# An S4 layer with a gated feed-forward net, forward and backward: powers only at the positions that bf16 leaves distinct, four channels per product, crossbar transposes, stored pre-activations

## The chip, the cores and the metric

The kernel runs on one core of one Trainium2 chip. The metric is the device time of one execution in microseconds (us). The engines are PE (matrix multiply, with its weight loads counted apart as PEld), DVE (vector engine), ACT (scalar engine), POOL, and SP, which here only issues DMAs. "Granted clock" is the share of full speed that PE was allowed; with a low one matmuls take longer.

## The reference

The forward function and the gradients of all its inputs are to be computed, for L = 2048 positions, D = 512 channels, N = 128 states and F = 1792 hidden units. Cut to what matters:

```python
def ssm(u, A, B, C, log_dt, Dskip):
    dt = exp(log_dt)[:, None]
    l  = arange(L).astype(bfloat16)                  # the argument turns on this line
    P  = exp((dt * A)[:, :, None] * l)               # complex powers, D x N x L
    K  = einsum("dn,dnl,dn->dl", C, P, dt * B).real  # convolution kernel, D x L
    y  = irfft(rfft(pad(u)) * rfft(pad(K)))[:L]      # causal convolution, padded to 4096
    return y + u * Dskip
xn  = layernorm(x)
out = x + ssm(xn, ...) * silu(silu(xn @ w1) @ w2)
# outputs: out, and the gradients of x, A, B, C, log_dt, Dskip, w1, w2
```

The positions are rounded to bf16, so not all 2048 are distinct: 0 to 256 are exact, then come steps of 2, 4 and 8, with 128 values each. 257 + 3 x 128 = 641 are left.

## The kernel before

It never stores the powers of all positions. It writes each power as a product of a table X (a coarse step) and a table Y (a fine step), and K is then a matmul over the states. Two channels share one 128-column product. The same tables are needed transposed for the backward pass, so PE transposes them, ACT and DVE evacuate the results, and they go through DRAM (XTD, YTD). Per group of eight channel pairs, 32 groups in all:

```python
    X = ck.tile([P, 4, QCH, 64, 2], BF16, name="Xc")
    outer_pform(nc, X, H["XH"], H["XL"], H["XLn"], c0, QCH)       # 4 DVE products
    for qb in range(0, QCH, 2):                                   # transposes of X, on PE
        pf = psum.tile([P, 2, 2, P], F32, name="pf_t")
        ...  nc.tensor.matmul(out=pf[:, qi, c, :], lhsT=X[:, 2 * c, qb + qi]..., rhs=k.ident[:], ...)
        nc.scalar.copy(out=XT[:, qb:qb + 2], in_=pf[:])           # XTf, on ACT
    nc.sync.dma_start(k.XTD[:, q0:q0 + QCH], XT[:])
    YY = ...; outer_cplx(nc, ck, YY[:, 0]..., ...)                # 6 DVE products
    ...  # transposes of YY (pt_t), evacuated by DVE (YTf), stored to YTD
    for qi in range(8):
        for m in range(4):
            nc.tensor.matmul(out=ps[:, qi]..., lhsT=X[:, m, q]..., rhs=YY[:, m // 2, q, 32:64, :]...)   # ps_k
    nc.scalar.activation(out=tmpP[:, 1, :, qa:qa + 8].rearrange("p j q -> p q j"), in_=ps[:, :, :, 1], ...)  # kf_tmpP
    nc.scalar.activation(out=tmpP[:, 0, :, qa:qa + 8].rearrange("p j q -> p q j"), in_=ps[:, :, :, 0], ...)
```

The convolution is a discrete Fourier transform (DFT) in two matmul steps with a transpose between them. In this kernel PE does that transpose:

```python
    ...                                         # first step: PSUM -> A (tile dftA)
    for c in range(2):
        for g0 in range(0, G, 8):
            pt = psumT.tile([P, 8, 128], BF16, name="pt_b")
            for gi in range(8):
                nc.tensor.transpose(out=pt[:, gi, :], in_=A[:, c, g0 + gi, :, :]..., identity=ident[:])
            EV(nc, B[:, c, g0:g0 + 8, :], pt[:])
    ...                                         # second step: B -> X
```

The backward pass of the feed-forward net computes the first product again and takes silu and tanh of it:

```python
    for dk in range(DK):
        nc.tensor.matmul(out=ps_h[:], lhsT=XNT[:, dk, t, :], rhs=W1[:, dk, fs], ...)     # ps_hb, 256 matmuls
    for dk in range(DK):
        nc.tensor.matmul(out=ps_da[:], lhsT=DOT_s[:, dk, :], rhs=W2T[:, dk, fs], ...)
    nc.scalar.activation(out=a_s[:, fs], in_=ps_h[:], func=ACT.Silu)
    nc.scalar.activation(out=th[:], in_=ps_h[:], func=ACT.Tanh, scale=0.5)
```

## Time and profile before

| | before |
|---|---|
| time, median of 2 | 1344.2 us (1342.22 to 1346.17) |
| profiled span | 1348.3 us |
| PE / DVE / ACT busy | 893 / 894 / 744 us |
| DMA packets, of which under 512 B | 333,686, 287,890 |

The page of the kernel before, parts 1 and 2. Part 1 gives busy time, share of the span and instructions of each engine. In part 2 each digit is the busy share, in tenths, of one of 40 equal slices of the span (33.7 us here); PEclk is the granted clock in tenths.

```profile
PE 893.1 (66%) x8258; PEld 580.6 (43%) x8314; DVE 894.4 (66%) x1490; ACT 744.2 (55%) x1217; POOL 9.4 (1%) x50
## 2 busy tenths in 40 slices
PE   1486850376767674666676666288788888646997
...
DVE  7177877597989894494756748187777777857100
ACT  5779887285646455547475565255555555541111
```

No engine is full on average. The limit changes with the stage, which the view by stretches shows. Its columns are the window and its length in us, then the busy us and the instructions of PE, PEld, DVE, ACT and POOL, the granted clock, the DMA share and GB/s.

```profile
0.00:255.00 255.00, 119.07 (x557) 55.34 (x568) 159.13 (x249) 192.15 (x279) 9.35 (x50) 0.85 0.28 102
255.00:520.00 265.00, 189.77 (x2700) 160.82 (x2701) 239.22 (x388) 157.84 (x216) 0.00 (x0) 0.85 0.50 154
520.00:849.00 329.00, 212.45 (x1940) 135.88 (x1959) 203.80 (x221) 189.46 (x304) 0.00 (x0) 0.87 0.26 59
849.00:1348.00 499.00, 371.81 (x3061) 228.51 (x3086) 292.28 (x633) 204.79 (x420) 0.00 (x0) 0.84 0.75 171
```

The first row is setup, the exponent tables and the feed-forward net. The second holds the tables: DVE is busy 239 of 265 us. The third holds the convolutions, where no engine passes 65%: a chain of steps that wait for each other. The fourth is the backward pass of the feed-forward net and of the state space model (SSM).

The groups view of the kernel before, for what the change removes. Columns: source line, engine, operation, output<-inputs, shapes, count | busy us, mean ns of one | idle us of the engine just before them, and what ended that idle time.

```profile
L620 PE MATMUL pf_t<-ident_bfloat_87,Xc 128*128 128x128 bf16 x512 | 84.4, 247 | 96.1 <-DVE Xc L344 72.9
L622 ACT CAST XTf<-pf_t 128x512 bf16<-128x512 f32 x128 | 74.0, 658 | 26.1 <-PE pf_t L621 12.5
L645 ACT ACTIVATE kf_tmpP<-ps_k,odd 128x256 bf16<-128x256 f32 x32 | 45.4, 1420 | 78.0 <-PE ps_k L642 76.5
L896 PE MATMUL ps_hb<-W_291,XNT 128*128 128x448 bf16 x256 | 60.7, 355 | 3.1 <-ACT Vb L779 1.9
```

The third line writes only 256 elements per partition and takes 1420 ns, while XTf writes 512 in 658 ns. kf_tmpP writes each element alone, far from the last one.

### The profile page before, as it was taken

Reading aid. Unit: us, or ns where it says so; the run is one execution under the profiler, and the core shown is the slowest. Engines: PE = TensorE matmul, PEld = TensorE weight load, DVE = VectorE, ACT = ScalarE, POOL = GpSimd, SP = SyncE. Lnnn points to the kernel's source line nnn. Section 1 sums busy time; section 2 is a strip of 40 time slices with the busy share of each in tenths; the row PEclk is TensorE's granted clock in tenths of the full one; section 3 lists DMA queues with packets and bytes.
Section 4 is the critical chain, followed back from the end, with each engine's and each line's share of the span. In section 5 each row is a group of like instructions: output and inputs, shape, how many; then the busy total and the mean of one; then the engine's idle time right before and its main releaser. Section 6 shows DMA issues by size and latency. Waiting matters only on the chain. (4 is left out here: it accounts for less than half of the span.)

```text
span 1348.3 us, 20797 instructions
## 1 busy us (share of the span) xinstructions
PE 893.1 (66%) x8258; PEld 580.6 (43%) x8314; DVE 894.4 (66%) x1490; ACT 744.2 (55%) x1217; POOL 9.4 (1%) x50
## 2 busy tenths in 40 slices
PE   1486850376767674666676666288788888646997
PEld 0232320266656563334354443144444444333487
DVE  7177877597989894494756748187777777857100
ACT  5779887285646455547475565255555555541111
POOL 0000000000000000000000000000000000000000
PEclk9999985587888887889898888598888898856999
DMA  3112312546463736442411102977686877897744
GB/s 129 59 62 86 133 67 89 206 158 210 125 195 103 204 110 146 97 94 47 94 33 32 32 1 46 221 160 184 150 185 153 178 168 180 156 171 211 176 130 117
DMA packets 333686, 171.90 MB, mean 127 GB/s; under 512 B 287890, under 2 KB 300052, under 8 KB 333076
## 3 DMA queue, kind: packets, MB, share of 16 engines
q1 hardware_dynamic: 179348, 102.65, 28.5%
q10 hardware_dynamic: 154240, 67.91, 20.3%
q8 instruction: 65, 1.06, 0.3%
q14 instruction: 33, 0.27, 0.1%
HBM read 93.19 MB, written 77.33 MB: 126 GB/s over the span
## 5 line engine op out<-in xcount | busy, mean ns | idle before, releaser
L620 PE MATMUL pf_t<-ident_bfloat_87,Xc 128*128 128x128 bf16 x512 | 84.4, 247 | 96.1 <-DVE Xc L344 72.9
L620 PEld LDWEIGHTS <-Xc 128*128 128x128 bf16 x512 | 54.3, 112 | 80.6 <-issue 69.9
L645 ACT ACTIVATE kf_tmpP<-ps_k,odd 128x256 bf16<-128x256 f32 x32 | 45.4, 1420 | 78.0 <-PE ps_k L642 76.5
L622 ACT CAST XTf<-pf_t 128x512 bf16<-128x512 f32 x128 | 74.0, 658 | 26.1 <-PE pf_t L621 12.5
L779 ACT CAST Vb<-psV 128x512 bf16<-128x512 f32 x128 | 67.1, 594 | 29.8 <-PE psV L777 23.3
L621 PE MATMUL pf_t<-ident_bfloat_87,Xc 128*128 128x128 bf16 x512 | 79.3, 245 | 4.2 <-DVE Xc L347 3.5
L922 PE MATMUL ps_dx<-W1T,dhT 128*128 128x512 bf16 x204 | 66.4, 472 | 7.0 <-ACT dhT L184 4.7
L770 DVE TENSOR_TENSOR Gbd<-Gt,MK 128x512 bf16<-128x512 bf16 x64 | 43.4, 687 | 37.5 <-PE psV L777 36.0
L621 PEld LDWEIGHTS <-Xc 128*128 128x128 bf16 x512 | 54.1, 112 | 31.9 <-issue 23.0
L524 PE MATMUL ps_h<-XNT,W_291 128*128 128x512 bf16 x217 | 55.8, 407 | 16.8 <-ACT th L538 9.5
L899 PE MATMUL ps_da<-W2T,DOT_s 128*128 128x448 bf16 x256 | 60.9, 358 | 7.8 <-ACT DOT_s L184 3.7
L633 PE MATMUL pt_t<-ident_bfloat_87,YY 128*64 128x128 bf16 x512 | 49.0, 252 | 23.5 <-DVE YY L331 14.1
L896 PE MATMUL ps_hb<-W_291,XNT 128*128 128x448 bf16 x256 | 60.7, 355 | 3.1 <-ACT Vb L779 1.9
L642 PE MATMUL ps_k<-YY,Xc 128*128 128x64 bf16 x1024 | 48.8, 207 | 15.4 <-ACT kf_tmpP L646 14.8
L646 ACT ACTIVATE kf_tmpP<-ps_k,even 128x256 bf16<-128x256 f32 x32 | 51.8, 1619 | 5.5 <-DVE YTf L634 5.5
L534 PE MATMUL ps_o<-W_440,aT 128*128 128x512 bf16 x220 | 49.8, 379 | 4.8 <-ACT aT L526 4.5
L633 PEld LDWEIGHTS <-YY 128*64 128x64 bf16 x512 | 38.3, 129 | 33.2 <-DVE YY L331 17.5
L777 PE MATMUL psV<-XT,Gbd 128*128 128x256 bf16 x256 | 48.6, 330 | 5.8 <-DVE Gbd L770 2.6
L642 PEld LDWEIGHTS <-Xc 128*128 128x128 bf16 x1024 | 42.8, 107 | 21.2 <-issue 16.9
L974 PEld LDWEIGHTS <-xn 128*128 128x128 bf16 x512 | 48.9, 98 | 4.1 <-issue 2.2
L114 PE MATMUL pt_b<-ident_bfloat_87,dftA 128*128 128x128 bf16 x384 | 31.5, 238 | 28.3 <-ACT dftA L26 14.8
L634 DVE COPY YTf<-pt_t 64x1024 bf16<-64x1024 bf16 x64 | 41.8, 680 | 11.9 <-PE pt_t L633 7.3
(2228 smaller groups left out, 2558.9 us busy)
## 6 DMA issues: line engine op xcount, KB each, us to landing
XTD<-XTf SPq DMA_DIRECT2D x32, 512.0 KB, 3.3
XT<-XTD SPq DMA_DIRECT2D x32, 512.0 KB, 4.3
YTD<-YTf ACTq DMA_DIRECT2D x32, 256.0 KB, 2.9
YT<-YTD SPq DMA_DIRECT2D x32, 256.0 KB, 4.0
YT<-YTD ACTq DMA_DIRECT2D x32, 256.0 KB, 4.8
Ad<-a_s SPq DMA_DIRECT2D x16, 448.0 KB, 3.3
DHd<-dh_s ACTq DMA_DIRECT2D x16, 448.0 KB, 4.3
A_ft<-Ad SPq DMA_DIRECT2D x7, 512.0 KB, 4.0
```

Source lines behind the costliest of these rows:

```text
L524: nc.tensor.matmul(out=ps[:], lhsT=W1[:, dk, ft * P:(ft + 1) * P], rhs=XNT[:, dk, 4 * tcn:4 * tcn + 4, :], start=(dk == 0), stop=(dk == DK ...
L534: nc.tensor.matmul(out=pso[:], lhsT=aT[:, ft, tt * P:(tt + 1) * P], rhs=W2[:, ft, :], start=(ft == 0), stop=(ft == FT - 1))
L620: nc.tensor.matmul(out=pf[:, qi, c, :], lhsT=X[:, 2 * c, qb + qi].rearrange("p a b -> p (a b)"), rhs=k.ident[:], start=True, stop=False)
L621: nc.tensor.matmul(out=pf[:, qi, c, :], lhsT=X[:, 2 * c + 1, qb + qi].rearrange("p a b -> p (a b)"), rhs=k.ident[:], start=False, stop=True)
L622: nc.scalar.copy(out=XT[:, qb:qb + 2], in_=pf[:])
L633: nc.tensor.transpose(out=pt[0:64, qi, c, :], in_=YY[:, c, qb + qi, 0:32, :].rearrange("p j e -> p (j e)"), identity=k.ident[:])
L642: nc.tensor.matmul(out=ps[:, qi].rearrange("p j e -> p (j e)"), lhsT=X[:, m, q].rearrange("p a b -> p (a b)"), rhs=YY[:, m // 2, q, 32:64, ...
L646: nc.scalar.activation(out=tmpP[:, 0, :, qa:qa + 8].rearrange("p j q -> p q j"), in_=ps[:, :, :, 0], func=ACT.Copy, scale=k.even[:, 0:1])
L779: nc.scalar.copy(out=Vb[:, qb:qb + 2], in_=psV[:])
L896: nc.tensor.matmul(out=ps_h[:], lhsT=XNT[:, dk, t, :], rhs=W1[:, dk, fs], start=(dk == 0), stop=(dk == DK - 1))
L899: nc.tensor.matmul(out=ps_da[:], lhsT=DOT_s[:, dk, :], rhs=W2T[:, dk, fs], start=(dk == 0), stop=(dk == DK - 1))
L922: nc.tensor.matmul(out=ps_dx[:], lhsT=dhT[:, ft, :], rhs=W1T[:, ft, :], start=(ft == 0), stop=(ft == FT - 1))
```

## The change

The intent is to do less of everything in the tables: powers at 641 positions only (21 coarse exponents E and 32 fine steps Y per channel), four channels in one 128-row product instead of two, no transposes on PE (the crossbar of the DMA does them, in the DFT too), no recomputed first product (pre-activations are stored and loaded), and a new form of the SSM sums. It is a rewrite; this is its core, with cuts marked:

```diff
+E_EXP = [256 * i for i in range(1, 9)] + list(range(8)) + [258, 260, 262, 516, 772]
+Y_EXP = [8 * j for j in range(1, 8)] + [64, 128, 192]
 ...  # gen_tables, per half block of 64 channels
-    outer_pform(nc, X, H["XH"], H["XL"], H["XLn"], c0, QCH)
-    ...  (pf_t, XTf, XTD; outer_cplx; pt_t, YTf, YTD)
+    V = tbl.tile([P, 2, 8, 64], I32, name="V", tag="tv")          # phase; single buffer
+    ...
+    nc.scalar.activation(out=sn[:, :, 0:n], in_=V[:, :, 0:n], func=ACT.Sin, ...)
+    TT(out=..E.., in0=qe(sn[...]), in1=qe(mag[...]), op=ALU.mult)
+    nc.sync.dma_start(k.Ed[b, h], E[:]...)
+    ...  # Y from its exponents, stored to Yd; W = E times C
+    for q in range(8):
+        for m in range(4):
+            nc.tensor.matmul(out=ps[:, q // 4, (q % 4) * 84:(q % 4) * 84 + 84],
+                             lhsT=Y[:, m // 2, q0 + q]..., rhs=W[:, m, q]..., start=(m == 0), stop=(m == 3))
+    for u in range(2):
+        k.evk(Xr[:, :, :, qq + 4 * u:qq + 4 * u + 4].rearrange("p a e q -> p q e a"),
+              ps[:, u, 0:336].rearrange("p (q e a) -> p q e a", e=NE, a=4))
 ...  # dft_fwd
-            for gi in range(8):
-                nc.tensor.transpose(out=pt[:, gi, :], in_=A[:, c, g, :, :]..., identity=ident[:])
-            EV(nc, B[:, c, g0:g0 + 8, :], pt[:])
+    nc.sync.dma_start_transpose(B[:].rearrange("p c g k -> p (c g) k"), A[:].rearrange("p c g t e -> p (c g t e)"))
 ...  # backward of the feed-forward net
-                nc.tensor.matmul(out=ps_h[:], lhsT=XNT[:, dk, t, :], rhs=W1[:, dk, fs], ...)
-            nc.scalar.activation(out=a_s[:, fs], in_=ps_h[:], func=ACT.Silu)
+                nc.sync.dma_start(sl[:, 0:n], k.Hd[2 * f:2 * f + n, :, 256 * c:256 * c + 256]...)
 ...  # results of the inverse DFT, four channels interleaved (du_b is written the same way)
+    nat = lambda ap: ap.rearrange("p t (q a) -> p t a q", a=4)
+    nc.vector.tensor_tensor(out=nat(S[:, t0:t0 + n])[:, us], in0=ps[:, us].rearrange("p t (a q) -> p t a q", a=4),
+                            in1=nat(xd[:])[:, us], op=ALU.add)
```

## The prediction

> **What bounds the kernel now.** No engine alone. The page's first part: of 1348 us PE is busy 893, DVE 894, ACT 744. The stretches view shows changing limits: DVE in 300-580 us (225 of 280 us; powers), nobody in the convolutions, about 515-849 us (PE 217, DVE 207, ACT 194 of 334: a serial chain), PE with DVE in 849-1170 us (PE 244, DVE 229 of 321), DMA waits in 1170-1230 us (chain of waits: six parameter loads, 34 us).
>
> **What goes.** By the groups view: transposing matmuls pf_t (164 us busy PE), pt_t (49), pt_b (32) and more, with evacuations XTf (ACT 74), YTf (DVE 42); table products Xc (DVE 87) and the XTD/YTD round trips; recomputed ps_hb (PE 61) with its second silu (ACT 35). kf_tmpP (ACT 97) is replaced by Xr.
>
> **What comes**, estimated from durations in the trace: two-source bf16 DVE at 2 elements per cycle (1024: 682 ns), fp32 or PSUM at 1 (512: 692 ns), one-source bf16 at 4 (448: 272 ns), ACT 0.19 us plus 0.83 ns per element, 0.216 us per 512-column matmul. Over the new instruction list:
> - PE 560 us, of which GEMMs 340 and 1344 64-column products psS 75.
> - DVE 750, of which powers (V, E, Y, W) 190, complex products 114, PSUM evacuations 78, T 55.
> - ACT 490 plus the evacuation Xr: 32 of 1344 elements, each written alone to another place (steps of 64 and 1344 bytes). The same kind of write, kf_tmpP, took 1420-1650 ns for 256 elements where a contiguous one would take about 490: some 4.5 ns per element. So Xr should take 6.2 us, 195 us in all, not 42. The Trainium skill (SBUF - State Buffer, Specifications) has 16-byte cachelines and a penalty for every crossing; this trace agrees for ACT.
> - DMA transposes, about 44 MB, unmeasured here. The skill (DMA: Bandwidth & Descriptors, Latency and other measured facts) has 261 GB/s; with our DMAs' landing time of 3-5 us, an estimate of 7 us for 1 MB (dB<-dA).
>
> **Critical path, by stage.**
> 1. Setup, tables, FFN and convolution forward: per 128 channels ACT 88, DVE 69; FFN adds ACT 70; start 30. ACT binds: about 490 us (DVE would at 400 were Xr cheap).
> 2. Gate and convolution backward: serial, one buffer each, 45-50 us per block, half of it complex products on DVE: 190.
> 3. da and first SSM block: PE 124, DVE 112: 145.
> 4. Weight gradients, layer norm, three SSM blocks: PE 175, DVE 155, 28 transposes: 205.
>
> Sum 1030 us. Predicted 1030 us, range 910 to 1150 (8 in 10). Faster by over 2%: 0.94; within 2%: 0.03; slower: 0.03.
>
> **What would show each step.** Groups view: Xr evacuation near 6 us and ACT the busiest engine until about 480 us; if near 1.3 us, the total falls to about 940. dB<-dA landing in 6-9 us. DVE busy near 750, ACT near 680. The stretch of gate and conv backward with DVE about 80% busy, PE below half, and a low granted clock. Packets under 512 B far below 287,890.
>
> **What would make it wrong.** Transposes much slower than plain copies: they all stand on one queue (SP), and a slow one delays every load and store behind it; at 20 us per MB the backward convolutions gain 50 us and weight gradients become DMA-bound. Single-buffered tables (V, sn, W) stalling DVE behind ACT's in-order Xr. In the other direction: Xr written cheaply, or the scheduler overlapping the backward convolutions with da more than I allow.

A note on its units. Its three DVE rates come out of the trace of the kernel before: beyond a fixed 0.16 us, one element costs 1.04 ns in fp32 (1536 elements take 1755 ns, 512 take 688), 0.51 ns with two bf16 sources (1024: 682 ns, 448: 387 ns), and, worked out from one size only, about 0.25 ns with one (448: 272 ns). Its "cycle" is the first of these. And 0.216 us is the distance from one matmul's start to the next (ten of ps_w end within 2.32 us), while a single one lasts 376 ns or more there, since they overlap.

## The result, and the profile after

| | before | after |
|---|---|---|
| time, median of 2 | 1344.2 us (1342.22 to 1346.17) | 1047.15 us (1044.91 to 1049.39) |
| ratio | | 0.7796 (95% interval 0.7742 to 0.7851) |
| PE / DVE / ACT busy | 893 / 894 / 744 us | 667 / 694 / 477 us |
| DMA packets under 512 B | 287,890 | 215,731 |

A ratio is the mean time of one kernel's fast runs over that of the other's of the same rounds, so it is not quite the ratio of the medians quoted beside it. The outputs are correct.

The page of the kernel after, parts 1 and 2 (a slice is 26.2 us):

```profile
PE 666.7 (64%) x5692; PEld 454.2 (43%) x5692; DVE 693.7 (66%) x1359; ACT 476.7 (46%) x643; POOL 9.8 (1%) x70
## 2 busy tenths in 40 slices
PE   0968789544515361455554546886899786777978
...
DVE  6757666658576676147596867696796586545755
ACT  0888876674147232633533232253436346522312
...
PEclk9989789856655675566667766898899889988989
```

The view by stretches of the kernel after, cut where my prediction cut it: (1) setup, tables, feed-forward net and forward convolutions; (2) gate and backward convolutions; (3) da and first SSM block; (4) weight gradients, layer norm and three SSM blocks.

```profile
0.00:490.00 490.00, 265.05 (x1928) 172.05 (x1929) 311.09 (x631) 266.24 (x407) 9.85 (x70) 0.74 0.48 132
490.00:702.00 212.00, 125.14 (x851) 83.54 (x850) 157.87 (x263) 74.93 (x73) 0.00 (x0) 0.72 0.49 134
702.00:825.00 123.00, 104.02 (x987) 73.77 (x988) 87.83 (x153) 55.07 (x54) 0.00 (x0) 0.94 0.67 168
825.00:1047.00 222.00, 172.47 (x1926) 124.83 (x1925) 136.88 (x315) 80.42 (x110) 0.00 (x0) 0.90 0.78 170
```

Two readings. The gain is shared evenly: everything up to the end of the convolutions took 849 us and takes 702 (147 less); the rest took 499 and takes 345 (154 less). And the first stretch lasts exactly the 490 us that I predicted, yet ACT, which I said would bind it, is busy for 266 of them. No engine binds it. DVE is at 63%, ACT and PE at 54%, and PE runs at 0.74 of its clock. This is a serial chain, as the convolutions were before.

The groups view of the kernel after shows which size was off. (Shapes are partitions x elements of one partition.)

```profile
L41 ACT CAST Xr<-ps_k 128x336 bf16<-128x336 f32 x32 | 49.8, 1807 | 35.5 <-PE ps_k L390 35.5
L253 PE MATMUL ps_s<-dB,F 128*128 128x512 bf16 x96 | 47.3, 493 | 81.9 <-DMA dB<-dA 77.4
```

And the same view with shapes kept apart:

```profile
L366 DVE TENSOR_TENSOR E<-sn,mag 128x512 bf16<-128x512 f32 x32 | 20.7, 689 | 37.7 <-ACT sn L359 37.7
L464 DVE TENSOR_TENSOR S_b<-ps_i,xd 128x512 bf16<-128x512 f32 x16 | 19.5, 1318 | 13.0 <-PE ps_i L273 12.6
```

An Xr evacuation has 336 elements, not the 1344 on which my 6.2 us rested. It takes 1807 ns. Taking off the 0.19 us of fixed cost that my prediction read from other ACT groups, that is 4.8 ns per element, close to the 4.5 predicted. The rate was right and the count was four times too high. S_b and du_b have the same flaw on DVE, which I had not seen: their 512 results are written alone, 8 bytes apart, and take 1318 ns, where the prediction's own rule for a PSUM source says 692.

What holds the stretch in place of ACT's load, from the view of waits of the kernel after, 200 to 490 us (after the feed-forward net has ended). Columns: engine, what it was about to run <- what ended its wait: us in all, times, longest.

```profile
PE ps_k L390 <- issue: 53.4, 3, 19.0
...
PE ps_s L253 <- DMA dB<-dA: 50.3, 6, 9.8
ACT sn L359 <- DVE V L357: 37.7, 15, 4.3
ACT Xr L41 <- PE ps_k L390: 32.4, 8, 9.0
...
DVE E L366 <- ACT sn L359: 24.7, 9, 4.4
```

In the first line, "issue" means that the profile shows nothing that PE waited for; in the longest of these gaps, which ends at 314 us, the timeline shows DVE and ACT making the next tables. So PE, ACT and DVE wait for one another, and PE waits for the transposing DMA. One such place, in the timeline of the kernel after (start us, busy us, instruction, and in brackets the idle time before it with its releaser):

```profile
295.22 3.06 ACT L41 CAST Xr<-ps_k 128x336 bf16<-128x336 f32 x2 [2.47 <-PE ps_k L390]
...
297.79 1.34 ACT L359 ACTIVATE sn<-V,pi 128x1024 f32<-128x1024 int32 x1
299.16 1.29 DVE L366 TENSOR_TENSOR E<-sn,mag 128x512 bf16<-128x512 f32 x2 [4.41 <-ACT sn L359]
```

ACT takes its instructions in the order of the program here. It waits 2.47 us for a product of this half block, spends 3.06 us on two Xr, and only then makes the sines for the next one, for which DVE has stood idle 4.41 us. So Xr costs little in load, but it is a link of a chain.

### The profile page after: what moved, and what is told of

Its sections match the earlier page's. It is cut to its first block, busy times and chain, and to the rows that moved or that the text cites. A ratio compares the mean times of both kernels' runs of the same rounds, so it can differ in the third digit from the quotient of the medians.

```text
span 1047.3 us, 14472 instructions
## 1 busy us (share of the span) xinstructions
PE 666.7 (64%) x5692; PEld 454.2 (43%) x5692; DVE 693.7 (66%) x1359; ACT 476.7 (46%) x643; POOL 9.8 (1%) x70
## 2 busy tenths in 40 slices
DMA packets 299001, 151.42 MB, mean 145 GB/s; under 512 B 215731, under 2 KB 286645, under 8 KB 295861
## 5 line engine op out<-in xcount | busy, mean ns | idle before, releaser
L253 PE MATMUL ps_s<-dB,F 128*128 128x512 bf16 x96 | 47.3, 493 | 81.9 <-DMA dB<-dA 77.4
L486 PE MATMUL ps_h<-XT,W 128*128 128x256 bf16 x448 | 57.0, 283 | 35.2 <-DMA XT<-xn 25.6
L744 PE MATMUL ps_w<-do,a_tok 128*128 128x512 bf16 x224 | 56.0, 410 | 23.5 <-ACT a_tok L741 23.4
L41 ACT CAST Xr<-ps_k 128x336 bf16<-128x336 f32 x32 | 49.8, 1807 | 35.5 <-PE ps_k L390 35.5
L486 PEld LDWEIGHTS <-W 128*128 128x128 bf16 x448 | 45.3, 102 | 44.1 <-issue 23.9
L762 PE MATMUL ps_w<-dh_tok,xn 128*128 128x256 bf16 x448 | 60.5, 287 | 5.4 <-DMA dh_tok<-DHd 5.4
L498 PE MATMUL ps_o<-W,aT 128*128 128x512 bf16 x224 | 56.6, 402 | 10.6 <-ACT hT L41 9.3
L718 PE MATMUL ps_da<-doT,W2T 128*128 128x256 bf16 x448 | 58.2, 288 | 6.7 <-DMA doT<-do 3.5
L631 DVE TENSOR_TENSOR T<-Vb,Eb 128x1344 bf16<-128x1344 bf16 x64 | 51.1, 853 | 6.0 <-ACT Vb L41 4.9
L718 PEld LDWEIGHTS <-W2T 128*128 128x128 bf16 x448 | 45.9, 103 | 15.9 <-issue 7.3
```

Source lines behind the costliest of these rows:

```text
L41: return self.nc.scalar.copy(out=out, in_=in_)
L253: nc.tensor.matmul(out=ps[:, 4 * u:4 * u + 4], lhsT=F2[:, m0], rhs=B[:, 0, g0:g0 + 4, :], start=True, stop=False)
L486: nc.tensor.matmul(out=ps[:, j], lhsT=k.W1[:, dk, ft * P:ft * P + P], rhs=XTv[:, :, dk, :], start=(dk == 0), stop=(dk == DK - 1))
L498: nc.tensor.matmul(out=ps[:], lhsT=aT[:, ft, t * P:t * P + P], rhs=k.W2[:, ft, :], start=(ft == 0), stop=(ft == FT - 1))
L631: TT(out=Tt[:, :, c].rearrange("p q w e a -> p q w (e a)"), in0=Vb[:, :, c], in1=Eq[:, ec].unsqueeze(2).to_broadcast([P, 8, 2, NE * 4]), o ...
L718: nc.tensor.matmul(out=ps[:, j], lhsT=W2T[:, dk, ft * P:ft * P + P], rhs=dTv[:, :, dk, :], start=(dk == 0), stop=(dk == DK - 1))
```

## The experiments

Two theories had to be told apart. **Load**: the first stretch is as long as it is because of the work of its busiest engine (DVE, 311 us). Then taking away a few tens of us of work elsewhere, or adding some, does about as much as its share of load. **Chain**: it is as long as the sum of the links of a serial chain. Then shortening a link helps by about its length, whoever runs it, and even if the engines get more to do. Alongside, I asked what each removed part was worth in the kernel before.

Kernels sent together share the runs of the kernel before on their chip. The median of its 7 runs was 1345.81 us for the first four below, 1345.76 for the next four (all at once, recompute, and the first two removals), 1341.6 for the evacuations, the products and all removals together, and 1345.28 for the mended one.

### The changed kernel again

> The changed kernel again, so that its variants are compared on one chip: 1047 us, within 0.5%.

No edit. 1044.35 us (1041.73 to 1045.59, 4 runs), ratio 0.7753 (0.7726 to 0.778). It is the yardstick for the next three.

### Write order of Xr, S_b and du_b

```diff
-                k.evk(Xr[:, :, :, qq + 4 * u:qq + 4 * u + 4].rearrange("p a e q -> p q e a"),
-                      ps[:, u, 0:336].rearrange("p (q e a) -> p q e a", e=NE, a=4))
+                k.evk(Xr[:, :, :, qq + 4 * u:qq + 4 * u + 4],
+                      ps[:, u, 0:336].rearrange("p (q e a) -> p a e q", e=NE, a=4))
 ...  # S_b; du_b alike
-            nc.vector.tensor_tensor(out=nat(S[:, t0:t0 + n])[:, us], in0=ps[:, us].rearrange("p t (a q) -> p t a q", a=4), in1=nat(xd[:])[:, us], ...)
+            nc.vector.tensor_tensor(out=S[...][:, us].rearrange("p t (q a) -> p t q a", a=4), in0=ps[:, us].rearrange("p t (a q) -> p t q a", a=4), in1=xd[:, us]..., ...)
```

The same elements go to the same places, in another order: Xr is written in runs of four neighbours, S_b and du_b without gaps, and the reads from PSUM jump instead. In S_b and du_b the second input, which lies in SBUF, is now read without gaps too.

> Three evacuations (Xr, S_b, du_b) walk the same elements in another order: runs of 4 neighbouring bf16 written, lone fp32 read from PSUM. If lone writes are what costs 4.8 ns per element, Xr falls from 1.81 to about 0.5 us (32 of them: ACT minus 42 us) and S_b and du_b from 1.31 to 0.69 us (32: DVE minus 20 us); if reading PSUM with a stride costs as much, all stay. Chain theory (stage 1 is one chain of waits; Xr, S_b and du_b lie on it): total falls by 40 to 60 us. Engine theory (my prediction: ACT or DVE is full in stage 1): ACT is only half busy there after 200 us, so only du_b and the FFN overlap gain, under 20 us.

1002.5 us (997.41 to 1009.76), ratio 0.7449 (0.7406 to 0.7492): 42 us less. The groups view of this kernel, shapes kept apart:

```profile
L41 ACT CAST Xr<-ps_k 128x336 bf16<-128x336 f32 x32 | 12.5, 441 | 38.3 <-PE ps_k L390 38.3
L464 DVE TENSOR_TENSOR S_b<-ps_i,xd 128x512 bf16<-128x512 f32 x16 | 10.3, 686 | 11.8 <-PE ps_i L273 11.5
L366 DVE TENSOR_TENSOR E<-sn,mag 128x512 bf16<-128x512 f32 x32 | 20.7, 688 | 23.8 <-ACT sn L359 23.8
```

Xr falls from 1807 to 441 ns and S_b from 1318 to 686. So for Xr the lone write was the cost, not the lone read from PSUM. For S_b and du_b it was the lone write or the equally scattered read of the second input; no run separates these. ACT's busy time fell by 35 us (477 to 442) and DVE's by only 17, and DVE is the busiest engine: under the load theory some 17 us could be gained, not 42. In the first stage DVE has only S_b's 9 us less to do, yet the last S_b starts at 457 us instead of 490. The wait of E for sn fell from 37.7 to 23.8 us. This speaks for the chain.

### A second buffer for the phase tile V

```diff
-            V = tbl.tile([P, 2, 8, 64], I32, name="V", tag="tv")
+            V = tbl.tile([P, 2, 8, 64], I32, name="V", tag="tv", bufs=2)
-            m1 = tbl.tile(shp, BF16, name="m1", tag="tv")
+            m1 = tbl.tile(shp, BF16, name="m1", tag="tv", bufs=2)
-    KE = tbl.tile([P, 8, 8, 32], BF16, name="KE", tag="KE")
+    KE = tbl.tile([P, 8, 8, 32], BF16, name="KE", tag="tv", bufs=2)
```

KE, of the same size, moves into the same two buffers, so that the second one needs no more memory. No instruction gets less to do.

> The phase tile V gets a second buffer, so DVE prepares the next exponents while ACT takes the sine of these. If the alternation V, sn, E is what stretches stage 1, the wait of E for sn (44 us) and of sn for V (42 us) mostly goes and the total falls by 25 to 45 us. If those waits come from ACT's order (Xr evacuations ahead of sn), or the convolution is the long part, under 10 us.

1016.89 us (1016.34 to 1018.3), ratio 0.7554 (0.7525 to 0.7584): 27 us less with nearly the same work (DVE is busy 687 us against 694, ACT 475 against 477). The wait of E for sn (128x512 form) fell from 37.7 to 27.0 us; I had expected most of it to go. The load theory gives 7 us at most here, so the chain is shown for this part.

### The transposes of the DFT on PE

```diff
-    nc.sync.dma_start_transpose(B[:].rearrange("p c g k -> p (c g) k"), A[:].rearrange("p c g t e -> p (c g t e)"))
+    for c in range(2):
+        pt = pc.tile([P, 16, P], BF16, name="pt_b", tag="pc")
+        for g in range(16):
+            nc.tensor.transpose(out=pt[:, g, :], in_=A[:, c, g, :, :].rearrange("p t e -> p (t e)"), identity=k.ident[:])
+        for h in range(2):
+            ev(B[:, c, 8 * h:8 * h + 8, :], pt[:, 8 * h:8 * h + 8, :])
```

> The twelve 1 MB crossbar transposes dB<-dA are undone: 384 transposes on PE and 48 evacuations of 1024 columns (ACT plus 33, DVE plus 11 us, PE plus 21 us). Intent of the change (crossbar relieves the engines): slower, by 15 to 45 us. Rival (each crossbar transpose stands 6.8 us on a serial chain; PE and the evacuations need about 5 us): the same or faster by up to 30 us. PE's wait of 77 us for dB goes in either case.

990.31 us (988.13 to 996.47), ratio 0.7362 (0.7327 to 0.7396): 54 us less, and above the 30 that even the rival allowed, though PE is busy 20 us more (689 against 669, with all 384 transposes) and ACT 28. Undoing this part of the change makes the kernel faster. The groups view of this kernel, shapes kept apart:

```profile
L258 PE MATMUL ps_s<-dB,F 128*128 128x512 bf16 x96 | 38.6, 402 | 14.5 <-ACT dB L41 5.9 <-DVE dB L42 4.4 <-ACT DS L41 2.1
...
L249 PE MATMUL pt_b<-ident,dA 128*128 128x128 bf16 x384 | 32.6, 260 | 7.0 <-DVE dA L42 4.8 <-ACT dA L41 2.0
...
L41 ACT COPY dB<-pt_b 128x1024 bf16<-128x1024 bf16 x30 | 28.9, 1016 | 17.6 <-PE pt_b L249 9.9 <-DVE dB L42 7.7
```

PE's wait before the second step fell from 81.9 to 14.5 us. And the matmuls behind it became shorter, 402 ns against 493, with PE idling less: in the timeline of the kernel after, when a wait of 8.16 us for dB ends at 247.34 us, the first seven take 0.61 to 0.63 us, and from 250.3 us on they take 0.38 to 0.40. The Trainium skill (TensorE: Matmul & The Clock Gate, Part 1) says that an idle window puts PE's clock at half. Granted clock rose from 0.798 to 0.841 with the waits taken away, which agrees.

The transposing DMA was not slower than a plain one. From the view of DMA issues of the kernel after (count, KB each where they are given, median us from issue to landing):

```profile
sp_in<-Ud SPq DMA_DIRECT2D x4, 1024.0 KB, 6.6
...
dB<-dA SPq DMA_TRANSPOSE x12, 6.8
```

One megabyte lands 6.8 us after its issue, against 6.6 us for a plain load of 1 MB. The Trainium skill (Advanced Engine Details and Errata, DMA Advanced Topics) says that "TRN2 transpose DMAs are as fast as regular DMAs", and in that sense the trace agrees. But the block's convolution has nothing else to run in these 6.8 us, twelve times over. Another page, VectorE: DVE Perf Modes, The three transpose paths, gives 390 ns for one 128x128 transpose on TensorE and 1309 ns on the crossbar, and its rules take TensorE where the result may land in PSUM. That advice held here. The 32 blocks of one DMA come to 6.8 / 32 = 0.21 us each. A transposing matmul lasts 260 ns here, but they overlap: all 384 keep PE busy for 32.6 us, 0.085 us each, and an evacuation of eight blocks takes 0.69 us on DVE or 1.02 on ACT. So PE has the better rate as well. What I take to be a second difference, without a run for it, is that PE's blocks come out one by one, so that evacuation and second step start on the first of them, while a DMA's blocks all come at the end.

PE's own balance accounts for less than half of the gain. It waited 81.9 us before the second step, and now spends 32.6 us on the transposes, 7.0 waiting for their inputs and 19.7 waiting before the second step (14.5, and 5.2 at the line after): 23 us less. Shorter matmuls and an SP queue without twelve long issues (see below) may be the rest; no run separates them.

The issue itself holds the queue as well. From the view of the tile dB in the kernel after (duration ns of the issuing instruction: least, median, most):

```profile
L246 SPq DMA_TRANSPOSE dB<-dA x12: 4712/4874/7112, 139.0 to 657.2; - x12
```

And the same of a plain load of 1 MB, the tile sp_in:

```profile
L436 SPq DMA_DIRECT2D sp_in<-Ud x4: 331/689/1091, 504.2 to 662.2; - x4
```

For 4.9 of the 6.8 us SP can issue nothing else.

### All three at once

The edit is the sum of the three above.

> The three single edits together (write order of Xr, S_b and du_b; two V/m1 buffers; PE transposes in the DFT). Alone they gained 42, 27 and 54 us on 1044. If the stage is a serial chain on which these are separate links, the gains add: 1044 - 123 = about 921 us. If all three only remove the same wait in different places, the gain is that of the best one: about 990 us. Between the two (920 to 990) means that part of the links are shared: the write order and the second buffer both shorten the wait of E for sn, so I expect these two to overlap, and the total near 935 us. Mean of the first-stage end (last S_b): 490 in the changed kernel, about 405 here.

929.76 us (929.64 to 931.48), correct, ratio 0.6916 (0.6899 to 0.6933), with 1345.76 us before on its chip. In ratios the single gains are 0.0304, 0.0199 and 0.0391, together 0.0894 below the 0.7753 of the changed kernel; measured is 0.0837, or 94% of the sum. So over the whole kernel the gains add, as for links of one chain (94% and 100% are not apart, given the intervals). In the first stage alone they overlap somewhat: the last S_b starts at 490.5 us in the changed kernel, at 457, 459 and 452 with the single edits and at 401 with all three, 89 us earlier where the sum is 104. The page of this kernel, part 1:

```profile
PE 675.9 (73%) x6076; PEld 475.7 (51%) x6076; DVE 674.6 (73%) x1375; ACT 468.3 (50%) x674; POOL 10.6 (1%) x70
```

And its group of E, from the groups view with shapes kept apart:

```profile
L371 DVE TENSOR_TENSOR E<-sn,mag 128x512 bf16<-128x512 f32 x32 | 20.6, 685 | 7.3 <-ACT sn L364 7.3
```

The sums of work are those of the kernel after, within 3%: PE 676 against 667, DVE 675 against 694, ACT 468 against 477. The time fell by 11%.

### Evacuations of the DFT moved off DVE

```diff
-    k.evc = Evac(nc, "AAD")        # one evacuation in three on DVE
+    k.evc = Evac(nc, "AAAAAD")     # one in six
```

> The combination e5_all with the evacuations of the DFTs moved from one in three on VectorE to one in six: DVE about 35 us less, ACT about 33 us more. If DVE load is now the limit in the first 585 us (it is busy 75 to 82% there), the total falls by 15 to 25 us from 930; if the serial chain of evacuations is, two evacuations in a row on ACT lengthen it and the total rises by 5 to 20 us; a change under 5 us tells neither apart.

923.4 us (922.37 to 926.3), ratio 0.6883 (0.6856 to 0.691); the intervals of this and the last kernel overlap. The gain is 6 us by the medians, which come from two chips, and 4 by the ratios. DVE fell by 42 us and ACT rose by 37. By its own terms the experiment tells nothing apart: the load moved as planned and the time hardly did.

### The recomputed product put back into the changed kernel

```diff
-                nc.sync.dma_start(sl[:, 0:n], k.Hd[2 * f:2 * f + n, ...])
+                for g in range(n // 2):
+                    ph = k.pf.tile([P, 2, 256], F32, name="ps_hb", tag="pf")
+                    for j in range(2):
+                        for dk in range(DK):
+                            nc.tensor.matmul(out=ph[:, j], lhsT=W2T[:, dk, ft * P:ft * P + P], rhs=dTv[:, :, dk, :], ...)
+                    k.evf(sl[:, 2 * g:2 * g + 2, :], ph[:])
```

> The changed kernel with the recomputed first product put back as a cost: in the da stage the pre-activations come from 448 matmuls of 256 columns on stand-in operands and ACT evacuations, not from a load of Hd; dW1 and dW2 come out wrong on purpose. If PE binds that stage (104 of 123 us busy), these 50 to 60 us of PE lie on the path: 1044 + 45 to 58 = 1090 to 1100 us. If the stage is a chain of waits with slack on PE, it stays within 15 us of 1044.

1119.03 us (1116.31 to 1123.03), ratio 0.833 (0.83 to 0.836): 75 us more, above the 45 to 58 expected. The view by stretches from the end of the convolutions on, first for the changed kernel run again, then for this one:

```profile
sum 342.00, PE 280.27 PEld 200.95 DVE 224.24 ACT 135.61 POOL 0.00; mean PE 140.14 PEld 100.47 DVE 112.12 ACT 67.81 POOL 0.00
```

```profile
sum 421.00, PE 341.13 PEld 247.93 DVE 236.66 ACT 174.76 POOL 0.00; mean PE 170.56 PEld 123.96 DVE 118.33 ACT 87.38 POOL 0.00
```

PE is busy 280 of 342 us, and 341 of 421: 82% and 81%. So 61 us more of PE work cost 79 us there, and the idle 18% of PE did not absorb it. That this part goes at PE's pace alone is not shown, for then it would be 61: the edit also puts 56 evacuations on ACT before silu (ACT is busy 39 us more, and waits 41 us for ps_hb), and no run separates the two. Storing the pre-activations was worth about 75 us in the changed kernel.

### The removed parts, one at a time, in the kernel before

Three edits of the kernel before, each taking one part away. Their outputs are wrong, which doesn't matter for the times.

No transposes of the tables:

```diff
-                        nc.tensor.matmul(out=pf[:, qi, c, :], lhsT=X[:, 2 * c, qb + qi]..., rhs=k.ident[:], ...)
-                nc.scalar.copy(out=XT[:, qb:qb + 2], in_=pf[:])
-            nc.sync.dma_start(k.XTD[:, q0:q0 + QCH], XT[:])
+            for c in range(2):
+                nc.sync.dma_start(k.XTD[:, q0:q0 + QCH, c], X[:, 2 * c].rearrange("p q a b -> p q (a b)"))
 ...  # and the same for pt_t, YTf, YTD
```

> The kernel before, without the transposing matmuls of its X and Y tables (pf_t, pt_t) and their evacuations (XTf, YTf); untransposed tiles are stored in their place, so the SSM gradients are wrong on purpose. Busy time falls by about 213 us of PE, 74 of ACT and 42 of DVE. My prediction counted these among what goes, but held that DVE binds the stretch at 300-580 us: then only the DVE part and the waits of DVE for PE are on the path, 40 to 80 us off 1345. If PE work there was the limit, it falls by over 130 us; if all hidden, under 20 us.

1303.19 us (1298.45 to 1306.52, median of the three fast runs), ratio 0.9686 (0.9648 to 0.9723): 43 us less, at the low end of the DVE account, for groups that in the kernel before keep PE busy 213 us and ACT 74. One of its four executions took 4043.87 us, and is left out. It was also the profiled one, so this kernel has no trace that can be compared. Its stand-in stores have the small runs that are mended further down, so the transposes may have been worth a little more.

No recomputed product:

```diff
+        nc.sync.dma_start(a_s[:], ...)                    # a stand-in of the same size is loaded
-            for dk in range(DK):
-                nc.tensor.matmul(out=ps_h[:], lhsT=XNT[:, dk, t, :], rhs=W1[:, dk, fs], ...)
-            nc.scalar.activation(out=a_s[:, fs], in_=ps_h[:], func=ACT.Silu)
 ...  # tanh reads a_s in place of ps_h
```

> The kernel before without the recomputed activations (ps_hb and the second silu; a stand-in is loaded; some outputs wrong on purpose). PE falls by about 61 us and ACT by 35. If PE binds the stretch at 1010-1170 us (115 of 128 and more), 45 to 61 us come off 1345; if DVE or the waits for loads bind, under 20 us.

1312.13 us (1310.03 to 1317.31), ratio 0.9761 (0.9729 to 0.9793): 34 us less. This lies between both expectations. The stand-in load is not free: from 849 us on the DMA share is 0.86, against 0.75 in the kernel before, so the product itself may have been worth more.

Products for one group in eight:

```diff
-            outer_pform(nc, X, H["XH"], H["XL"], H["XLn"], c0, QCH)
+            if c0 == 0:
+                ... outer_pform(nc, X, H["XH"], H["XL"], H["XLn"], c0, QCH)
 ...  # and the same for outer_cplx
```

> The kernel before with the complex products of its tables (Xc and YY with their temporaries, ten instructions of 0.68 us per group of eight channel pairs) computed for the first of every eight groups only and used again for the other seven; wrong on purpose. DVE falls by 7/8 of 32 x 10 x 0.68 = 190 us. In the stretch of the tables, 255-530 us, DVE is now busy 242 of 275 us, PE 192 and ACT 161. If DVE is what bounds that stretch, it shrinks until PE binds: 60 to 80 us off 1345. If the stretch is a chain of waits for which all three engines count, it shrinks by more than that, 100 us or over; if DVE was not the limit, by under 30 us.

1300.69 us (1295.61 to 1303.34) with 1341.6 before, ratio 0.9686 (0.9644 to 0.9727): 41 us less, between the expectations, for 169 us less of DVE work (894 to 726). The stretch of the tables in this kernel, from the view by stretches:

```profile
255.00:474.00 219.00, 158.80 (x2686) 146.44 (x2685) 69.29 (x106) 156.60 (x213) 0.00 (x0) 0.90 0.60 183
```

DVE was busy for 239 of the 265 us, and is busy for 69 of 219. So DVE did bind, but by little: right behind it came a chain of PE, ACT and the stores of the transposed tables. PE and ACT are at 72% each, and in the view of waits DVE's YTf waits 74 us for PE's transposes and 45 us for the stores of YTD, ACT's XTf 34 us for those of XTD.

All three together, and once more with the stand-in stores mended:

```diff
-            for c in range(2):
-                nc.sync.dma_start(k.XTD[:, q0:q0 + QCH, c], X[:, 2 * c].rearrange("p q a b -> p q (a b)"))
+            nc.sync.dma_start(k.XTD[:, q0:q0 + QCH].rearrange("p q c n -> p (q c n)"), X[:, 0:2].rearrange("p m q a b -> p (m q a b)"))
```

What I expected of the three together, and then of the mended version:

> The kernel before with all three removals at once: no table transposes, no recomputed activations, products for one group in eight; wrong on purpose. Alone the first two gave 41 and 34 us. Removing transposes and products together takes away both DVE's and PE's work in the table stretch, which leaves ACT's kf_tmpP (97 us) there: if my account of what binds holds, the stretch falls from 275 to 110 us and the total to about 1345 - 165 - 34 = 1146 us, more than the three gains added. If gains merely add, the total is 1345 - 41 - 34 - what the products alone give. What is left between this and 1044 us is then owed to the rest of the rewrite (conv spectra on four channels, loads, order), since the changed kernel still computes its powers.

> b4_none with one flaw of it mended: my stand-in stores of XTD and YTD went out in 256-byte runs (429,156 packets, DMA share 1.06 in the table stretch of 154 us), where the kernel before stores 4 KB runs. Here they go out in 4 KB runs, as before (order wrong on purpose). If those stores held the stretch in b4_none, it shrinks from 154 to about 110 us, bound by ACT's kf_tmpP (97 us), and the total falls from 1201 to about 1155 us. If the stretch was held by the waits of products for the loads of H (54 us of Xc <- H_XH) whatever the packets, the total stays within 15 us of 1201.

The first gave 1201.41 us (1199.67 to 1203.08), ratio 0.8954 (0.8914 to 0.8993): 140 us less, more than the 118 of the single gains, as my account of limits says, but far from 1146. Its stores in 256-byte runs made me doubt it. The second gave 1194.39 us (1191.85 to 1195.96), ratio 0.8874 (0.8846 to 0.8902): within 15 us of the first, so the small runs were not what held it, and my 1155 missed. The stretch of the tables in the second:

```profile
255.00:395.00 140.00, 42.64 (x1044) 40.72 (x1045) 29.40 (x43) 72.11 (x65) 0.00 (x0) 0.65 0.94 285
```

No engine passes 52%, but the DMA share is 0.94, and the first product of a block waits 35 us in all for the load of H_XH. With the engines' work gone, the DMA traffic is likely the next limit; no run took it away.

## Why the prediction was right or wrong

**The total: right, and by luck in its largest term.** 1030 us were predicted and 1047 measured, within the range.

**"ACT binds: about 490 us": this step failed.** The stretch lasts 490 us, but ACT is busy for 266 us of it. The term that was mis-sized is Xr: "32 of 1344 elements ... 6.2 us, 195 us in all". It has 336 elements, takes 1.8 us, and costs 49.8 us in all. The rate per lone element (4.5 predicted, 4.8 measured) was right. The alternative, "if near 1.3 us, the total falls to about 940", failed as well: it took DVE's load as the limit and left out the chain. With all three links shortened the kernel does come to 930 us, but DVE is then busy 304 of the first 405 us, 75%, so it is not full there either. What I had listed only as a danger ("Single-buffered tables (V, sn, W) stalling DVE behind ACT's in-order Xr") turned out to be one of the links: the second buffer for V alone gained 27 us. Two errors cancelled: some 145 us too much ACT load, and no wait for V, for Xr and for the transposes (shortening these three brought the end of the stage forward by 89 us).

**"dB<-dA landing in 6-9 us": right (6.8), and under-used.** I costed the transposes as landing times and then worried only about slower ones. Even at the predicted speed, taking them out gained 54 us; the waits of PE account for 23 of these.

**S_b and du_b:** my rule for PSUM sources (512 elements: 692 ns) missed the scattered order; 1318 ns. I looked for them on ACT and not on DVE.

**Stage 2, "190":** 212 measured. DVE is busy 158 us, 74%, not quite the "about 80%"; PE is above half (125 of 212, at a clock of 0.72), not below. With the three links mended the same stage, 405 to 585 us, takes 180 us with DVE at 148 (82%).

**Stages 3 and 4, "145" and "205":** 123 and 222, together 345 against 350. PE is the busiest engine there, as predicted (104 of 123 us, 172 of 222), and adding 61 us of PE work added 79 us, evacuations included.

**Loads:** PE 560 predicted, 667 measured. The big products came out as predicted (342 us against 340, the sum of six groups); the rest took 107 us more than I had allowed. The DFT matmuls are among it, at a clock of 0.72 to 0.74 in the first two stages; how much of the 107 us the clock explains, no run shows. DVE: 750 predicted, 694 measured. ACT: 685 predicted, 477 measured; Xr is 145 of these 208 us, and the rest I can't account for.

**"Packets under 512 B far below 287,890": wrong.** 215,731 is a quarter less.

**What goes:** the transposes of the tables, 213 us of PE, were worth 43 us. Recomputing was worth 34 us in the kernel before, and 75 us when put into the changed kernel. The products were worth 41 us. All three together were worth 140 to 151 us.

**What stays open.** From the 1194 us of the kernel before with all three parts gone to the 1044 of the changed kernel there are 150 us more, although the changed kernel still computes its powers. By stretches, about 35 lie before the end of the convolutions (737 against 702 us) and about 112 after it (457 against 345). Of the second part I tested nothing alone: the removed transposes of dh, the new SSM sums, and the earlier parameter loads all fall in it.

## What to carry to other kernels

Count the elements of one instruction from its access pattern before costing it, and then ask of each stage whether its busiest engine is nearly full: where PE was at 82%, 61 us more of its work (and the evacuations that came with it) cost 79, but where DVE was at 63%, the links of the chain counted, whether a lone write on ACT, a missing buffer or a DMA, and their gains added to 94%. An operation that is free as throughput, such as a transpose inside a DMA, is not free where the next step can do nothing but wait for it. The best kernels shorten all three links, are correct, and take about 930 us, or 923 with fewer evacuations on DVE (a difference that the intervals don't confirm), against 1047 and 1344.

## What the Trainium skill lacked or had wrong

- SBUF — State Buffer, Specifications, says that each crossing to a new cacheline pays a penalty, without a size. Here a lone bf16 write cost 4.8 ns per element on ACT (1807 ns for 336, against 441 written in runs of four), and on DVE 512 results took 1318 ns written 8 bytes apart, with one input read in the same order, against 686 without gaps. Reading the PSUM side in the jumping order cost neither engine anything that shows: 441 and 686 ns are the reads of lone fp32 elements.
- DMA: Bandwidth & Descriptors, Rules for kernel authors, names the crossbar for a transpose during DMA, without what the issue costs. Elsewhere the page has issue times for a transpose, in sequencer cycles, but only in a comparison of a later chip with "previous generations". Here the issue occupied SP for 4.87 us (median) for 1 MB, and for 8.05 and 12.35 us in the transposing loads of w1 and w2, against 0.69 us for a plain load of 1 MB.
- VectorE: DVE Perf Modes, The three transpose paths, compares single transposes (390 against 1309 ns); 32 in one DMA came to 0.21 us each, and 384 on PE kept it busy for 0.085 us each. No page that I used says what the choice is worth on a serial chain: 54 us for twelve transposes of 1 MB, with 384 transposes on PE in their place.
- TensorE: Matmul & The Clock Gate, Part 1, warns that recorded clock events are not always reliable, and tells of a clock stuck at a quarter for 50 us and more. One execution of 4043.87 us may be of this kind, and longer: a 448-column matmul took 1539 ns on average over the whole execution, against 358 in the kernel before (4.3 times), while the record gave a granted clock of 1.0.
